# VectorE instead of GpSimd for one expert's weight split, and the last attention unit turned on TensorE instead of by DMA

## The chip, the cores and the metric

The kernel runs on one core of a Trainium2 chip. The metric is the device time of one execution in microseconds (us). The core has engines that work side by side, each through its own instructions in the order of the program: TensorE (PE; its weight loads are listed as PEld), VectorE (DVE), ScalarE (ACT), GpSimd (POOL) and SyncE (SP), which issues most DMAs. An engine waits for another by semaphores.

## The reference

Three layers in a row, in float32, on 4 batches of 576 tokens. The first is causal attention with 8 heads of 64 and a bias of cumulated decays. The second is a mixture of 8 experts: each token goes to one expert, its own best or, where a gate is open, that of the token in front of it. The third is a gated convolution layer of width 1024.

```python
x = attn_out.transpose(0, 2, 1, 3).reshape(B, S, H * D)          # 4 x 576 x 512
logits = einsum('bsd,de->bse', x, w_gate)                        # 8 experts
local_gate = 1 / (1 + exp(-einsum('bsd,de->bse', x, w_local)))
for b, s:                                                        # in order of s
    fresh_e = argmax(logits[b, s])
    e = fresh_e if s == 0 or local_gate[b, s] < 0.5 else prev_e
    out[b, s] = softmax(logits[b, s])[e] * (maximum(x[b, s] @ w1[e], 0) @ w2[e])
# then h = relu(out @ w_in); c = conv3(h); (h * sigmoid(c)) @ w_out
```

## The kernel before

Float32 values are split into a high and a low half of 16 bits, and a product is three matmuls (high by high, high by low, low by high). Everything is emitted by hand in one order, so each engine takes its instructions in the order of the program.

**Attention** runs in 8 units (4 heads of one batch each), and a unit in 14 steps; `at(d)` in its loop names what is d steps behind. For step t: scores (PE), `weights` one step behind (ACT exp), `rest` two (DVE), `values` four (PE, L503), `norm` five (DVE, L541), `xout` six (DVE, L547). A unit's result has two parts of two heads. `store` splits a part into halves `xh`: the high by ACT (L559), the low by DVE (L560) for the last unit. `rt.turn` turns them, so that the feature stands on the partitions: a DMA transpose issued by SP (L824), for the tail tokens another (L827). `put` writes them to `xd` in DRAM. For the last unit (NU - 1 = 7), part 0 is stored, turned and put at step N + 1 (N = 112 steps in all), part 1 at N + 6 and N + 7. values of its last head come at step N + 3 and the logits of unit 6 at N + 1, behind the turn of part 0 in the code.

**Routing.** `logits` (PE, L838 and L843) takes a turned unit, `collect` (DVE, L851 and behind) its logits; `finish` does both for the last unit, then the tables: exp (ACT, L899), sums (L900), the scan over the tokens (L905) that hands an expert on to the next token, positions (L920 to L934), one-hot planes (`plane`, L944), `sums` on PE into the PSUM tile `ix` (L954), and from it the tokens of each block of 128 (`rows(0)`, L960, for the gathers), the rows to write (`rows(1)`) and the scale `pp` (L981 to L983). `warm` (L964) puts matmuls without use between.

**The experts' weights** come expert by expert: `load(w, e)` by SP from DRAM into a stage (w is 0 for w1, 1 for w2; expert e; four parts), `lead` makes the high halves (ACT, L1023), `rest` the low ones: on DVE (one instruction, L1034) or, with `pool=True`, on GpSimd (two, L1030 and L1032). A part of a stage can be loaded anew when its `rest` is done. Four calls of these stand between attention and `finish`: lead and rest of (0,0), lead of (1,0), rest of (1,0) with `pool=True`; then the loads (0,2) and (1,2). Behind `finish`: lead (1,1) and (0,2), rest (0,1) and (0,2) on DVE; rest (1,1), called `second`, on GpSimd in pieces between the gathers of the first four blocks.

**The experts' blocks** (`step(b)`). `gather(b)` fetches 128 tokens (GpSimd, L1101), `turn(b)` turns them (PE L1108 into the PSUM tile `xp`, ACT L1109 copies it to `xt`), `mm1` is 2 x 12 matmuls into two of four `hp` tiles (L1078), ACT takes the relu's high halves (L1123), DVE the low (L1124), and SP turns them by DMA transpose (`ht`, L1126); `mm2` follows three blocks later. In step 1 stand lead and rest of (1,2); in step 0, behind mm1, load(0,3). `refill` (SP, a branch at L1071) and `event` (ACT and DVE, a branch at L1062) bring the later experts.

PSUM: the routing's tiles z, nrp, rfp, ep, rk and ix take 1, 2, 2, 1, 1 and 1 banks in this order; the experts' tiles lie in the same eight: hp 4, yp 2, and xp the last two, which were those of rk and ix. A tile waits for the last user of what lay there.

Of the kernel before, what the change touches and what calls it, by code (L numbers as in the profile page):

```python
# [9 lines left out]
F32 = mybir.dt.float32  # L10
# [14 lines left out]
NU = B * H // NH  # L25
# [89 lines left out]
def attention(tc, ctx, q, k, v, s, xd, rt, hook):  # L115
# [545 lines left out]
    for t in range(N + 9):  # L661
        if t == N - 2 * PER - 6:
            early.close()
        for f in am:
            f()
        am = []
        work(t)
        at = lambda d: steps[t - d] if 0 <= t - d < N else None
        if at(0):
            scores(at(0))  # L670
        for u, i in pieces.get(t, ()):
            if i == 0:
                P[u] = stage_a(u)
            am.append(P[u][i]())
        if at(1):
            weights(at(1))
        if at(2):
            rest(at(2))
        for d, f in ((4, values), (5, norm), (6, xout)):
            y = at(d)  # L680
            if y and y[2] == (3 if y[1] % 2 else 2):
                f(y[0], y[1])
        y = at(7)
        if y and y[2] == 3 and y != (NU - 1, 1, 3):
            store(y[0], y[1] // 2)
        y = at(8)
        if y and y[1:] == (3, 3):
            u = y[0]
            rt.turn(u, U[u, "xh"], U[u // 2, "xth"] if u % 2 else None, range(2) if u < NU - 1 else range(1, 2))
            if u == NU - 1:  # L690
                put(u, range(1, 2))
        y = at(PAR["h"]["ps"])
        if y and y[1:] == (3, 3) and y[0] < NU - 1:
            put(y[0], range(2))
        if at(9) == (NU - 1, 1, 3):
            store(NU - 1, 0)
            rt.turn(NU - 1, U[NU - 1, "xh"], None, range(1))
            put(NU - 1, range(1))
        y = at(PAR['h']['lg'])
        if y and y[1:] == (3, 3) and y[0] < NU - 1:  # L700
            rt.logits(y[0], mps.tile([128, 512], F32, name="mt"))
        y = at(PAR['h']['lg'] + PAR['h']['co'])
        if y and y[1:] == (3, 3) and y[0] < NU - 1:
            rt.collect(y[0])
        hook(t)


class Routing:
# [110 lines left out]
    def turn(self, u, xh, xth, parts):  # L819
# [5 lines left out]
        if xth is not None:  # L825
            t = self.xp.tile([128, 2, 2, 128], F16, name="xTt", bufs=1)
            nc.sync.dma_start_transpose(out=t.rearrange("d x k t -> d (x k) t"), in_=xth.rearrange("p x m d -> p (x m d)"))  # L827
            self.X[u] = x, t

    def logits(self, u, z):  # L830
        PE = self.tc.nc.tensor
        x, t = self.X.pop(u)
        z = self.X[u] = z[:, 0:45].rearrange("p (i e) -> p i e", e=9)
        terms = ((0, 0), (0, 1), (1, 0))
        for c in range(2):
            for i in range(4):
                for n, (a, w) in enumerate(terms):
                    PE.matmul(z[:, i], lhsT=x[:, c, i, a], rhs=self.w[:, w, 2 * (u % 2) + c], start=i + c + n == 0, stop=c == 1 and n == 2, skip_group_check=True)  # L838
        if u % 2:
            for e in range(2):  # L840
                for k in range(2):
                    for n, (a, w) in enumerate(terms):
                        PE.matmul(z[0:64, 4], lhsT=t[:, a, k, 64 * e:64 * e + 64], rhs=self.wt[:, w, k, e], start=False, stop=e + k + n == 4, skip_group_check=True)  # L843
# [28 lines left out]
        V.tensor_reduce(fc, eq, axis=AX.X, op=ALU.max)  # L872
        V.tensor_tensor(self.zrf[:, :, b, 0:1], r, fc, op=ALU.mult)

    def finish(self, ctx, busy, between):

        nc, keep = self.tc.nc, self.keep
        V, A, PE, G = nc.vector, nc.scalar, nc.tensor, nc.gpsimd
# [64 lines left out]
        def plane(i, x):  # L943
            V.tensor_tensor(BQ[:, i], BQ[:, 1], bc(pairs(x), [128, 10, NB, 2]), op=ALU.mult)  # L944
# [17 lines left out]
        def warm(n):  # L962
            for _ in range(n):
                PE.matmul(z, lhsT=self.id16, rhs=busy, start=True, stop=True, skip_group_check=True)  # L964
# [9 lines left out]
        V.tensor_tensor(pl, pc, ph, op=ALU.subtract)  # L974
        for i, x in ((2, tok[:, 1]), (3, ph[:, :, 0]), (4, pl[:, :, 0])):
            plane(i, x)
        warm(PAR["r"]["w1"])
        sums(slice(2, 5))
        warm(PAR["r"]["w2"])
# [366 lines left out]
def attn_moe_moe2(tc, q, k, v, s, wg, wl, w1, w2, w_in, conv, w_out, out):  # L1346
    nc = tc.nc
    w_in, conv, w_out = (t.bitcast(I32) for t in (w_in, conv, w_out))
    with tc.manual_schedule(), ExitStack() as ctx:
        const = ctx.enter_context(tc.tile_pool(name="keep", bufs=1))  # L1350
        dram = ctx.enter_context(tc.tile_pool(name="mid", bufs=1, space=bass.MemoryType.DRAM))
        xd = dram.tile([NT + 128, 2 * DM], F16, name="xd")
        yd = dram.tile([NT + 128, 2 * DM], F16, name="yd")
        keep = Keep()
        keep.idx = const.tile([128, 2, NB], I32, name="idx")
        keep.unit = const.tile([128, 128], F16, name="unit")
        keep.pp = const.tile([128, NB], F32, name="pp")
        keep.tab = const.tile([1, 6, 32], I32, name="tab")
        keep.pscale = YS * 2.0 ** -8 * 2.0 ** -23
        c2, c3, cx, ce = ExitStack(), ExitStack(), ExitStack(), ExitStack()  # L1360
        lay = Keep()

        def hook(t):
            if t == -1:
                stg = c2.enter_context(tc.tile_pool(name="stg", bufs=1, side="right", reuse_waits="tile"))
                t1, t2 = stg.tile([128, 4, 1024], F32, name="st1"), stg.tile([128, 8, 512], F32, name="st2")
                lay.e0 = [t1[:, k:k + 1] for k in range(4)], [t2[:, 2 * k:2 * k + 2] for k in range(4)]
                lay.e1 = [], []
                lay.m = moe_weights(tc, w1, w2, keep, lay.e0)
                lay.m.whole = t1, t2  # L1370
                rt.open(cx)
                lay.st2 = ce.enter_context(tc.tile_pool(name="st2", bufs=4, side="right", reuse_waits="tile"))
                return t1, t2, lay.st2
            if t == PAR["h"]["rc"]:
                lay.steps = itertools.chain(rt.constants(wg, wl), (None,)), rt.weights()
            if PAR["h"]["rc"] <= t < PAR["h"]["rc"] + 80:
                for x in range(PAR["h"]["rk"] if t > PAR["h"]["rc"] else 1):
                    next(lay.steps[0], None)
                if t >= PAR["h"]["rc"] + 3:
                    next(lay.steps[1], None)  # L1380
            for i in range(4):
                if t == PAR["h"]["e"][i]:
                    lay.m.load(i % 2, 0, part=i // 2)
                if t == PAR["h"]["e1"][i]:
                    x = lay.st2.tile([128, 2, 2, 1024], F16, name="k2").rearrange("d e n c -> d (e n c)").bitcast(F32)
                    n = 1024 if i < 2 else 512
                    lay.e1[i // 2].extend(x[:, 1024 * j:1024 * j + 1024].rearrange("p (k f) -> p k f", f=n) for j in range(2))
                    lay.m.load(i // 2, 1, lay.e1[i // 2], i % 2)


        rt = Routing(tc, keep)
        attention(tc, c3, q, k, v, s, xd, rt, hook)
        c3.close()
        with ExitStack() as c4:
            rg = c4.enter_context(tc.tile_pool(name="rg", bufs=1, reuse_waits="tile"))
            r1 = rg.tile([128, 2, 4, 3, 1024], F16, name="r1")
            r2 = rg.tile([128, 2, 8, 3, 512], F16, name="r2")
            xgp, xtp = (c4.enter_context(tc.tile_pool(name=n, bufs=b, reuse_waits="tile")) for n, b in (("xg", 4), ("xt", 2)))
            m = lay.m
            m.rings = r1, r2  # L1400
            m.first(m.lead, 0, 0)
            m.first(m.rest, 0, 0)
            m.first(m.lead, 1, 0)
            m.first(m.rest, 1, 0, pool=True)
            m.load(0, 2)
            m.load(1, 2)
            with ExitStack() as c5:
                rt.finish(c5, r1[:, 0, 0, 0, 0:512], lambda: m.first(m.lead, 0, 1, lay.e1[0]))
            m.first(m.lead, 1, 1, lay.e1[1])
            m.first(m.lead, 0, 2)  # L1410
            m.first(m.rest, 0, 1, lay.e1[0])
            m.first(m.rest, 0, 2)

            def second(k):
                m.first(m.rest, 1, 1, lay.e1[1], pool=True, chunks=k)

            def weights():
                ce.close()
                cx.close()
                wpool = c2.enter_context(tc.tile_pool(name="w2", bufs=1, side="right", reuse_waits="tile"))  # L1420
                lay.wio = wpool.tile([128, 2, 4, 1024], F16, name="wi"), wpool.tile([128, 2, 8, 512], F16, name="wo")
                return lay.wio

            moe(tc, xd, yd, m, w_in, w_out, keep, second, weights, xgp, xtp, keep.unit)
        wi, wo = lay.wio
        moe2(tc, yd, conv, (wi, wo), out)
        c2.close()
# [29 lines left out]
```

## Time and profile before

| | us |
|---|---|
| median of 3 runs | 740.72 |
| lowest and highest | 740.4 and 742.1 |
| the profiled execution | 738.07 |
| its span, first to last instruction | 736.3 |
| busy in it: PE, DVE, ACT, POOL | 625.4, 443.8, 380.8, 251.2 |

The rows below come from the profiled execution alone. All times in them count from the first instruction. A row of a timeline is one or several like instructions in a row of one engine (xN), with the time from the start of the first to the end of the last, and in brackets how long the engine had been idle and what ended it. A letter q behind an engine's name (SPq) is its queue: an instruction that issues a DMA and is not counted as work.

### The profile page before, as it was taken

Reading aid. Unit: us, or ns where it says so; the run is one execution under the profiler, and the core shown is the slowest. Engines: PE = TensorE matmul, PEld = TensorE weight load, DVE = VectorE, ACT = ScalarE, POOL = GpSimd, SP = SyncE. Lnnn points to the kernel's source line nnn. Section 1 sums busy time; section 2 is a strip of 40 time slices with the busy share of each in tenths; the row PEclk is TensorE's granted clock in tenths of the full one; section 3 lists DMA queues with packets and bytes.
Section 4 is the critical chain, followed back from the end, with each engine's and each line's share of the span. In section 5 each row is a group of like instructions: output and inputs, shape, how many; then the busy total and the mean of one; then the engine's idle time right before and its main releaser. Section 6 shows DMA issues by size and latency. Waiting matters only on the chain. (4 is left out here: it accounts for less than half of the span.)

```text
span 736.3 us, 15742 instructions
## 1 busy us (share of the span) xinstructions
PE 625.4 (85%) x5301; PEld 383.7 (52%) x5301; DVE 443.8 (60%) x838; ACT 380.8 (52%) x640; POOL 251.2 (34%) x367
## 2 busy tenths in 40 slices
PE   0449659978988944799999999999879999999997
PEld 0226547756767832344444444444347776665443
DVE  5527447866867688963686849574109995455000
ACT  4134557756757974544564727352109985455110
POOL 9316656654534147932253443533200000000000
PEclk9999779998989965999999999999999999999999
DMA  9977688979768895399999998966256300000111
GB/s 183 203 134 140 159 157 162 131 169 184 130 142 223 262 256 192 81 270 287 228 271 347 233 283 180 264 151 127 69 105 118 54 2 29 30 16 28 58 44 57
DMA packets 197279, 113.37 MB, mean 154 GB/s; under 512 B 147286, under 2 KB 173182, under 8 KB 197182
## 3 DMA queue, kind: packets, MB, share of 16 engines
q1 hardware_dynamic: 192574, 99.14, 59.4%
q0 software_dynamic: 4272, 12.93, 5.9%
q8 instruction: 48, 0.79, 0.4%
q14 instruction: 49, 0.40, 0.2%
q10 hardware_dynamic: 336, 0.11, 0.1%
HBM read 62.20 MB, written 15.31 MB: 105 GB/s over the span
## 5 line engine op out<-in xcount | busy, mean ns | idle before, releaser
L1078 PE MATMUL hp<-r,xt 128*128 x504 | 112.2, 379 | 7.3 <-ACT xt L1109 7.3
L1078 PE MATMUL yp<-r,ht 128*128 x504 | 112.2, 379 | 1.7 <-PEq L1186 1.1
L334 DVE TENSOR_REDUCE mx<-za 128x1 f32<-128x512 f32 (+4 forms) x113 | 67.9, 615 | 56.5 <-PE za L331 55.8
L1270 PE MATMUL hp<-yt,wi 128*128 128x288 f16 x768 | 95.5, 286 | 2.8 <-DMA yt<-yd 2.8
L1318 PE MATMUL o<-wo,g 128*128 128x512 f16 x432 | 94.5, 379 | 0.0
L475 ACT ACTIVATE phi<-z,lnes 128x512 f16<-128x512 f32 (+1 forms) x104 | 65.6, 630 | 45.1 <-PE z L441 44.8
L1270 PEld LDWEIGHTS <-wi 128*128 128x128 f16 x768 | 75.1, 98 | 23.5 <-DMA yt<-yd 3.3
L1078 PEld LDWEIGHTS <-xt 128*128 128x128 f16 x504 | 49.2, 98 | 66.6 <-ACT xt L1109 8.4
L1078 PEld LDWEIGHTS <-ht 128*128 128x128 f16 x504 | 48.5, 98 | 57.4 <-issue 1.8
L1034 DVE SCALAR_TENSOR_TENSOR r<-st,r 128x512 f32 (+3 forms) x76 | 69.3, 980 | 11.7 <-ACT r L1023 5.7
L331 PE MATMUL za<-k 70*128 70x256 f16 (+2 forms) x160 | 39.6, 331 | 40.7 <-DMA k<-k 38.2
L1023 ACT ACTIVATE r<-st 128x512 f32 (+3 forms) x84 | 57.0, 761 | 27.5 <-SPq L1071 16.1
L438 PE MATMUL z<-k 71*128 71x256 f16 (+2 forms) x320 | 58.6, 302 | 14.2 <-DMA k<-mr 11.0
L487 DVE TENSOR_TENSOR plo<-z,phi 128x512 f16<-128x512 f32 (+1 forms) x104 | 63.2, 609 | 9.4 <-ACT z L476 9.3
L1318 PEld LDWEIGHTS <-g 128*128 128x128 f16 x432 | 42.3, 98 | 49.5
L1139 POOL DMA_INDIRECT yd<-ys,idx x21 | 21.5, 1025 | 133.2 <-DVEq L1062 89.5
L476 ACT ACTIVATE z<-z,lnes 128x512 f32<-128x512 f32 (+1 forms) x104 | 62.8, 604 | 0.0
L503 PEld LDWEIGHTS <-phi 128*128 128x128 f16 (+2 forms) x896 | 52.6, 107 | 4.9 <-issue 1.0
L503 PE MATMUL o<-vv,phi 128*128 128x65 f16 (+1 forms) x832 | 53.6, 202 | 0.0
L438 PEld LDWEIGHTS <-k 71*128 71x128 f16 x576 | 39.8, 105 | 25.6 <-DMA k<-mr 11.8
L503 PE MATMUL o<-vv,plo 128*128 128x65 f16 (+1 forms) x416 | 50.4, 199 | 0.0
L1287 DVE SCALAR_TENSOR_TENSOR c<-hb,cw,c 128x576 f32<-128x576 f32 x32 | 26.1, 815 | 35.0 <-ACT c L1281 35.0
(255 smaller groups left out, 1003.3 us busy)
## 6 DMA issues: line engine op xcount, KB each, us to landing
st<-in_moe_w_dram SPq DMA_DIRECT2D x8, 2048.0 KB
st<-in_moe_w_dram SPq DMA_DIRECT2D x24, 512.0 KB
out_dram<-s SPq DMA_DIRECT2D x18, 256.0 KB
st<-in_k_dram SPq DMA_DIRECT2D x16, 256.0 KB
st<-in_q_dram SPq DMA_DIRECT2D x16, 256.0 KB
k<-k SPq DMA_DIRECT2D x16, 256.0 KB
xd<-xh SPq DMA_DIRECT2D x16, 256.0 KB
k<-in_moe_w_dram SPq DMA_DIRECT2D x8, 512.0 KB
```

What stands on the lines that cost most here:

```text
L331: PE.matmul(out, lhsT=l, rhs=r, start=start, stop=stop, skip_group_check=True)
L334: return lambda: V.tensor_reduce(out, z.rearrange("p (e c) -> p e c", e=m), axis=AX.X, op=ALU.max)
L438: PE.matmul(out, lhsT=ks[i], rhs=qs[i], start=first and not i, stop=False, skip_group_check=True)
L475: A.activation(hi[:, 0:n], z[:, 0:n], AF.Exp, bias=lnes, scale=1.0 / SC)
L476: A.activation(p[:, 0:n], z[:, 0:n], AF.Exp, bias=lnes, scale=1.0 / SC)
L487: (V if md == "a" else G).tensor_tensor(lo[:, 0:n], p[:, 0:n], hi[:, 0:n], op=ALU.subtract)
L503: PE.matmul(out, lhsT=w, rhs=x, start=first, stop=last, skip_group_check=True)
L1023: i = self.nc.scalar.activation(hi, src, AF.Copy, scale=self.scale[w])
L1034: i = nc.vector.scalar_tensor_tensor(lo, in0=src, scalar=sc, in1=hi, op0=ALU.mult, op1=ALU.subtract)
L1078: i = self.nc.tensor.matmul(out, lhsT=lhsT, rhs=self.rings[w][:, c, k, bass.ds(s, 1), f], **kw)
L1270: PE.matmul(st[x][:, n, 0:HN], lhsT=wi[:, c, k, m], rhs=t[:, n, a + k], start=k + a + c == 0, stop=k == 3 and a == 4)
L1318: PE.matmul(o, lhsT=g[:, a, k, 128 * i:128 * i + 128], rhs=wo[:, c, k], start=j == 0, stop=j == 23)
```

## The change

`rest` of (1,0) is made by DVE and not by GpSimd, and it is no longer called ahead of `finish` but inside it, through a new argument `behind`, after the last `plane`. load(1,2), which refills the same stage, moves with it; load(0,2) stays. On DVE it is one instruction for each of 8 chunks, where GpSimd had two.

The last unit is turned by a new function `turn_last`: for each of two groups (the high halves, the low halves) four matmuls with a unit matrix into one tile of attention's PSUM pool `zps`, and a copy into `xT`, by ACT for the first and by DVE for the second. Part 1 has a third tile for the tail tokens, copied by ACT. It is called where `rt.turn` was.

```diff
         if y and y[1:] == (3, 3):
             u = y[0]
-            rt.turn(u, U[u, "xh"], U[u // 2, "xth"] if u % 2 else None, range(2) if u < NU - 1 else range(1, 2))
-            if u == NU - 1:
+            if u < NU - 1:
+                rt.turn(u, U[u, "xh"], U[u // 2, "xth"] if u % 2 else None, range(2))
+            else:
+                rt.turn_last(U[u, "xh"], U[u // 2, "xth"], 1, zps)
                 put(u, range(1, 2))
...
             store(NU - 1, 0)
-            rt.turn(NU - 1, U[NU - 1, "xh"], None, range(1))
+            rt.turn_last(U[NU - 1, "xh"], None, 0, zps)
             put(NU - 1, range(1))
...
+    def turn_last(self, xh, xth, part, pool):
+
+        nc = self.tc.nc
+        if NU - 1 not in self.X:
+            self.X[NU - 1] = self.xp.tile([128, 2, 4, 2, 128], F16, name="xT"), None
+        x = self.X[NU - 1][0]
+
+        def tile(blocks, out, copy):
+            z = pool.tile([128, 512], F32, name="z").rearrange("p (i t) -> p i t", t=128)
+            for i, b in enumerate(blocks):
+                nc.tensor.matmul(z[:, i], lhsT=b, rhs=self.id16, start=i == 0, stop=i == 3, skip_group_check=True)
+            copy(out, z)
+
+        copies = lambda o, z: nc.scalar.activation(o, z, AF.Copy), nc.vector.tensor_copy
+        for n in range(2):
+            tile([xh[:, part, i, n] for i in range(4)], x[:, part, :, n], copies[n])
+        if xth is not None:
+            t = self.xp.tile([128, 2, 2, 128], F16, name="xTt", bufs=1)
+            h = xth.rearrange("p x m d -> p (x m d)")
+            tile([h[:, 128 * i:128 * i + 128] for i in range(4)], t.rearrange("d x k t -> d (x k) t"), copies[0])
+            self.X[NU - 1] = x, t
...
-    def finish(self, ctx, busy, between):
+    def finish(self, ctx, busy, between, behind):
...
         for i, x in ((2, tok[:, 1]), (3, ph[:, :, 0]), (4, pl[:, :, 0])):
             plane(i, x)
+        behind()
         warm(PAR["r"]["w1"])
...
             m.first(m.lead, 1, 0)
-            m.first(m.rest, 1, 0, pool=True)
             m.load(0, 2)
-            m.load(1, 2)
             with ExitStack() as c5:
-                rt.finish(c5, r1[:, 0, 0, 0, 0:512], lambda: m.first(m.lead, 0, 1, lay.e1[0]))
+                rt.finish(c5, r1[:, 0, 0, 0, 0:512], lambda: m.first(m.lead, 0, 1, lay.e1[0]), lambda: (m.first(m.rest, 1, 0), m.load(1, 2)))
```

## Rows read from the trace of the kernel before

**Rows 1.** Busy time by stretch: length, busy us and instructions per engine, clock, DMA share, GB/s.
```profile
262.00:264.00 2.00, 0.00 (x0) 0.00 (x0) 1.46 (x4) 1.72 (x3) 0.00 (x0) 0.85 1.27 134
...
295.00:330.00 35.00, 29.52 (x165) 14.47 (x163) 29.27 (x28) 17.90 (x26) 23.12 (x18) 1.00 0.71 172
330.00:360.00 30.00, 30.00 (x158) 14.27 (x157) 11.76 (x18) 12.24 (x17) 8.14 (x10) 1.00 0.98 279
```

**Rows 2.** Timeline at 329: start, us, engine, line, operation, tiles, count, idle before.
```profile
329.29 5.34 PE L1078 MATMUL hp<-r,xt 128*128 x24 [0.45 <-ACT xt L1109]
```

**Rows 3.** Timelines of PE, ACT and DVE at the end of attention.
```profile
258.26 0.74 PE L838 MATMUL mt<-w,xT 128*128 128x9 f16 x24
...
258.77 0.66 ACT L559 ACTIVATE xh<-x 128x512 f16<-128x512 f32 x1
...
259.93 0.68 DVE L560 TENSOR_TENSOR xh<-x,xh 128x512 f16<-128x512 f32 x1
...
261.39 0.17 DVE L541 TENSOR_SCALAR rc<-o 128x5 f32<-128x5 f32 x1 [0.68 <-PE o L503]
```

**Rows 4.** Timeline from the last unit's halves to the scan.
```profile
263.12 8.04 ACT L1023 ACTIVATE r<-st 128x1024 f16<-128x1024 f32 x12
...
264.19 4.63 DVE L1034 SCALAR_TENSOR_TENSOR r<-st,r 128x1024 f16<-128x1024 f32 x4 [0.22 <-ACT r L1023]
264.41 1.82 SPq L824 DMA_TRANSPOSE xT<-xh  x1
...
269.11 0.81 PE L843 MATMUL z<-wt,xTt 128*64 128x9 f16 x12
...
269.95 0.20 DVE L851 SCALAR_TENSOR_TENSOR lgs<-z,lgs 128x36 f32<-128x36 f32 x1 [1.13 <-PE z L843]
...
274.49 1.29 DVE L905 TENSOR_TENSOR_SCAN er<-nrs,rfp 128x576 f16<-128x576 f32 x1
```

**Rows 5.** Timeline of the routing's tables, GpSimd's split beside VectorE's work.
```profile
271.24 1.16 POOL L1032 TENSOR_TENSOR r<-st,r 128x512 f16<-128x512 f32 x1
271.30 1.16 DVE L871 TENSOR_TENSOR eqf<-eqf,w 128x40 f32<-128x40 f32 x1
...
278.70 0.32 DVE L925 TENSOR_TENSOR inc<-inc,rk 128x160 f32<-128x160 f32 x1
...
280.78 1.28 DVE L929 TENSOR_TENSOR inc<-inc,oh 128x160 f32<-128x160 f32 x1
...
282.79 1.03 DVE L932 TENSOR_SCALAR at<-posi 128x20 int32<-128x20 int32 x1
```

**Rows 6.** Timeline from the last planes to the first block's turn.
```profile
289.54 0.43 DVE L944 TENSOR_TENSOR bq<-bq,pl 128x500 f16<-128x500 f16 x1
...
290.51 0.63 POOL L1030 TENSOR_SCALAR k<-k 128x512 f32<-128x512 f32 x1
...
292.78 0.18 DVE L982 TENSOR_TENSOR ixs<-ixs,ix 128x25 f32<-128x25 f32 x1
...
294.86 0.61 PE L1108 MATMUL xp<-unit,xg 128*128 128x128 f16 x8
```

**Rows 7.** Timeline of the first blocks: relu's low halves, SP's issues, ScalarE's event.
```profile
306.31 1.27 DVE L1124 SCALAR_TENSOR_TENSOR hs<-hp,hs 128x512 f16<-128x512 f32 x2
...
309.64 2.43 SPq L1042 DMA_DIRECT2D st<-in_moe_w_dram  x4
...
317.73 8.61 SPq L1126 DMA_TRANSPOSE ht<-hs  x2
...
323.37 3.90 ACT L1023 ACTIVATE r<-st 128x1024 f32 x4 [5.64 <-SPq L1071]
```

**Rows 8.** One line over the whole run: durations in ns, min, median and max.
```profile
L871 DVE TENSOR_TENSOR eqf<-eqf,w x4: 200/201/1155, 145.3 to 271.3; 128x40 f32<-128x40 f32 x4
```

**Rows 9.** Timelines of VectorE: eight low halves of this shape at two places.
```profile
307.81 8.65 DVE L1034 SCALAR_TENSOR_TENSOR r<-st,r 128x512 f16<-128x512 f32 x8 [0.21 <-ACT r L1023]
...
365.26 4.90 DVE L1034 SCALAR_TENSOR_TENSOR r<-st,r 128x512 f32 x8
```

## The prediction

> **What bounds the kernel now.** I read TensorE's busy time by stretch first [rows 1]. From 330 us on it is full: 30.00 of 30.00 us in the stretch shown, at the full clock. Whatever reaches that stretch later or earlier should therefore reach the end by as much. So the change is worth what it moves at the door of it, and I follow one instruction there: the first matmul of mm1(4), at 329.29 [rows 2], which still waited for ScalarE (0.45 us idle). In front of it (295 to 330) TensorE has 29.52 of 35 us, so some lateness can hide there. The second view is the timeline of 256 to 296 us, engine by engine: the end of attention [rows 3], the hand-over to the routing [rows 4], its tables [rows 5], the start of the experts [rows 6]. There is no resource that is full in it; it is one chain through in-order engines, mostly VectorE, and both edits lie on it.
>
> **Turning part 0 on TensorE.** The call stands at step N+1, ahead of the logits of unit 6 in the same step and of values(3) in step N+3. An engine takes its instructions in the order of the program, so these wait behind the turn. TensorE was free for the logits at 258.26 [rows 3]. The turn needs the high half, written by ScalarE at 258.77 + 0.66 = 259.43, and the low half, by VectorE at 259.93 + 0.68 = 260.61. Its two tiles are four matmuls each. No such matmul stands at this place; the nearest row is the eight alike of the experts' turn, 0.61 us [rows 6], so 0.35 a tile (bounds 0.3, and 0.7 at the half clock). The logits start at 260.66 + 0.35 = 261.0, not 258.26: 2.75 us late. The values behind them, which ended just before VectorE's normalisation at 261.39, end as much later, near 264.1. What went in its place, a DMA transpose, was hidden: its logits had the time of part 1 to wait.
>
> **Turning part 1.** Everything behind the values moves by 2.75: both halves of part 1 and of its tail are ready at 266.7. Then come two tiles and the tail's tile, each 0.35 on TensorE and 0.6 to 0.65 in the copy out of PSUM (nearest row: VectorE's 0.64 mean of the two relus' low halves from PSUM [rows 7]). ScalarE copies the first and the tail's, which ends near 267.8; the copy stands ahead of the first expert's high halves (lead(0,0)), which started at 263.12 [rows 4]. So ScalarE starts them 4.7 late. The low halves rest(0,0) on VectorE follow 1.07 behind, as before (264.19 against 263.12), take 4.63, and end at 267.8 + 1.07 + 4.63 = 273.5. Before, they ran while the transposes were under way and cost nothing; that cover is gone. The logits themselves are done at 269.0 to 269.2, against 269.11 + 0.81 = 269.92: 0.8 to 0.9 earlier. But collect (L851) is behind rest(0,0) on VectorE: it starts at 273.4, not 269.95. **+3.5 us.** Bounds: -0.9 if the logits alone decided, +4.5 with the turns at the half clock.
>
> Here a page is weighed. The row: from the issue of part 1's transpose at 264.41 to the tail's logits at 269.11 there are 4.7 us [rows 4], with 4.63 us of VectorE's work beside it. The Trainium skill, "VectorE: DVE Perf Modes", section "The three transpose paths", gives 390 ns on TensorE and 1309 ns by DMA for a 128 x 128 block. For part 1's 8 blocks and the tail's 4 that would be, as an estimate from that page, 12 x 0.92 = 11 us saved, a time near 730. The trace has the whole DMA route at 4.7 us and not 15.7, so there are not 11 us to save, and the order of VectorE decides here.
>
> **GpSimd's split leaves the routing.** GpSimd's L1032 starts at 271.24 and takes 1.16; VectorE's L871, 40 elements, starts at 271.30 and takes 1.16, ending with it. That is in [rows 5]; of the line's four executions the median is 0.20 [rows 8]. So while GpSimd reads its operands, such a VectorE instruction stands still. Eight do so between 270.6 and 283.8, the first big one L871 and the last L932 (1.03 us): L868, L871 and L901 lose 0.4, 0.95 and 0.85 (2.2 us) ahead of the scan L905, and L920, L926, L927, L929 and L932 lose 0.35, 0.7, 0.35, 0.95 and 0.85 (3.2) behind it. L929 is the plain case: 1.28 where L925, of the same shape, takes 0.32. All of that goes.
>
> Ahead of the scan it isn't all gained: ScalarE's exp, which the sum L900 needs, follows twelve high halves (263.12 to 271.16 before), now from 267.8 to 275.8. Exp and the copy nrs behind it, some 0.9 together, end near 276.7, and there the scan starts, not at 274.49: +2.2. Behind the scan -3.2 (and some 0.1 of small rows): the token lists, gathers and planes come **1.1 us early**. Bounds: -5.5 (collect at the logits, all eight free) and +1.
>
> **VectorE's eight new instructions.** They start behind the last plane, 289.54 + 0.43 = 289.97 [rows 6] (times from here on are on the clock of before, with the 1.1 to take off at the end). VectorE then idled 2.3 us for the sums, which hides that much. Eight of this shape take 4.90 us with nothing of GpSimd's beside them, and 8.65 beside its splits [rows 9]. GpSimd's own split of the second expert (second) starts at 290.51 [rows 6], so I take a value near the upper end: 8.2, that is to 298.2. With the four rows of rows(1) and pp behind it VectorE is free for rest(0,1) at 299.3, not 293.2: **6.1 us late** (2.6 and 6.5 at the two bounds).
>
> Three things stand behind this queue.
> First a wait that the diff doesn't show: the experts' xp tile takes the two PSUM banks of rk and ix, and the last reader of ix is L982. It was at 292.78, out of the way of xp's first matmul at 294.86, when the warming matmuls were through. Now L982 comes near 298.9, so TensorE starts its turn(0) at 299.0: 4.1 late.
> Second, the low halves of the relu (L1124), at 306.31 [rows 7]: between them and rows(1) VectorE had no idle time, so they go to 312.4. The transpose of ht(0) waits for them, and load(0,3), behind it on SP, goes from 309.64 to 315.9: 6.3 late. The load's bytes then keep the issue of ht(1)'s transpose (317.73) busy, and only behind that does SP pass the refill's branch for which ScalarE's event(0,3) at 323.37 had waited. I move that by the load: +6.3 (if the transpose's wait for L1124 of block 1 alone counts, +4.4, since GpSimd's split ends meanwhile and eight low halves run at the faster pace).
> Third, load(1,2) itself: its four parts are issued as VectorE frees them, 291.7 to 298.2, and no longer as GpSimd does, during the tables. Nothing but the gathers moves beside them then, so I take them as landed by 302; ScalarE comes to them in step 1, behind the first relus. Cost nothing, with an estimated 2 us in hand.
>
> ScalarE's event feeds xt(4), and that the matmul at 329.29. TensorE's own path (299.0 plus the same work as before, 294.86 to 329.29) gives 333.4 and a little more if the clock falls in the pause; ScalarE's gives 335.6 to 335.8. The later one counts: **+6.5**. Less 1.1: **+5.4 us**. The profiled execution was 738.07 (span 736.3 and 1.8 around it), so it would be 743.5; against the median of the runs shown, 740.72, which lies 2.65 above the profiled one, 746.1.
>
> **Rivals.**
> *VectorE falls behind less* (chance 0.15). The new instructions run at the pace of 4.90, as they would if GpSimd's split came later or the two didn't meet. Lag 2.6, xp at 295.5, the event +2.6: with -1.1 it is +1.5 to +3, 742 to 744. Against it: second follows two gathers directly, at 290.51.
> *The clock falls* (0.10). With xp waiting for L982, TensorE pauses 4 us ahead of mm1(0). The granted clock dropped from its upper level (2.4 GHz) to 1.2 in the stretch 262 to 264 [rows 1] (mean 0.85), after TensorE had been idle from 261.4, so such a pause may be enough. mm1(0) and part of mm1(1) would then take twice as long; if some 6 us run at half, 3 us are lost on TensorE's path: 333.4 + 3 = 336.4, and a second fall in the wait of mm1(4) adds as much again: +8 to +9, 749.
> *The front's gain cancels the lag* (0.08): collect follows the logits at 269.0, which gives -5.5 at the token lists, and the lag of 6.4 comes on top: +0.9, no change that can be told.
> *Faster* (0.12): the freed tables win. Place: VectorE's collect at 269; price: -5.5; then a lag of 2.6: -2.9, 737.8. It decides as soon as L851 starts before 270 and rows(1) ends by 296 (on the clock of before). For it speaks that those 5.5 us are plain in [rows 5] and that TensorE has 5.5 idle us from 295 to 330. Against it: the order on TensorE, ScalarE and VectorE puts values(3), lead(0,0) and rest(0,0) behind the turns, and nothing in the diff moves them.
> That the change doesn't do what it says I see no way to: both edits are plain moves.
>
> **How the numbers follow.** The forecast, +4 to +7 us, has 0.55. About 0.2% (1.5 us) is what a measurement of this kernel can tell from no change. Slower by more than that: forecast 0.55, smaller lag 0.15, clock 0.10, together 0.80; within it 0.08; faster 0.12. The likeliest time is 746.1; its own range is 744.5 to 748. To hold 8 of 10 it must take in the smaller lag, and half of the fallen clock: 740 to 750. What is left out is the faster case and the far end of the clock's.
>
> **What the profile after would show.** Right: values(3) ends near 264.1; L851 starts near 273.4 behind the low halves; no VectorE instruction of the tables takes 1 us; the token list L960 comes about 1 us early; the eight new instructions take about 8 us; xp's first matmul waits for VectorE (L982); load(0,3) and the event are 4 to 6 us later. Wrong: L851 at 270 or before; xp's first matmul directly behind the warming ones; mm1(4) within 1.5 us of 329.29; or an idle stretch of TensorE after 330 that was not there, by which the lateness would be given back or grow.

## The result, and the profile after

The changed kernel takes 744.65 us, the median of 20 runs; the kernel before, run on the same chip, 740.22 us, also of 20. The ratio is 1.0079, with a 95% interval of 1.0053 to 1.0105: 5.8 us slower on 740.2 (3.9 to 7.8). The ratio leaves out runs in a slower state of the chip, so it isn't the ratio of the two medians, which lie 4.4 us apart. The forecast was +5.4, that is 746.1 us. The profiled execution took 748.8 us (span 747.1).

To compare two traces I align their clocks at one VectorE instruction that precedes every edit, the normalisation (L541) of the last unit's last head but one: 259.11 us in the kernel before, 259.96 after. "Late" below means: later than before, so aligned. Differences under 1 us mean little: in the seven kernels below that keep both DMA turns, and so are alike up to collect, collect lies between 0.3 us early and 0.7 late.

First the stretches, as in [rows 1]: length, busy us and instructions of PE, PEld, DVE, ACT and POOL, granted clock, DMA share, GB/s.

```profile
260.00:262.00 2.00, 0.89 (x10) 0.72 (x11) 1.42 (x6) 0.87 (x2) 0.00 (x0) 0.68 1.04 394
262.00:264.00 2.00, 2.00 (x53) 2.00 (x50) 0.82 (x2) 0.00 (x0) 0.00 (x0) 0.50 1.07 371
264.00:266.00 2.00, 2.00 (x33) 1.77 (x31) 0.00 (x0) 0.00 (x0) 0.00 (x0) 0.50 0.98 291
...
300.00:305.00 5.00, 2.26 (x12) 1.27 (x13) 4.90 (x8) 1.02 (x1) 4.65 (x5) 0.67 0.89 280
305.00:310.00 5.00, 5.00 (x17) 1.86 (x15) 5.00 (x4) 0.60 (x1) 4.92 (x3) 0.65 0.08 34
...
330.00:360.00 30.00, 30.00 (x159) 14.30 (x157) 16.66 (x22) 15.30 (x20) 4.86 (x4) 1.00 1.01 264
```

TensorE is full again from 330 us on, at the full clock. In two places ahead of that it has much to do at a lower granted clock: 0.50 in 262 to 266 (0.50 is 1.2 GHz, 1.00 is 2.4 GHz), and a mean of 0.67 and 0.65 in the two stretches from 300 to 310. The kernel before has 0.50 from 264 to 294 too; but there the values of the last head, which end at 261.4, were through by then.

The timelines at the first place, where [rows 3, 4] stand for the kernel before. Columns: start, us, engine, line, operation, tiles, count, and in brackets the idle time ahead and what ended it.

```profile
260.32 0.23 PEld L842 LDWEIGHTS <-xh 128*128 128x128 f16 x4 [1.18 <-ACT xh L559]
260.33 0.40 PE L842 MATMUL z<-unit,xh 128*128 128x128 f16 x4 [1.06 <-DVE rc L542]
260.77 0.68 DVE L560 TENSOR_TENSOR xh<-x,xh 128x512 f16<-128x512 f32 x1
261.51 0.61 PE L842 MATMUL z<-unit,xh 128*128 128x128 f16 x4 [0.78 <-DVE xh L560]
261.91 0.83 PE L862 MATMUL mt<-w,xT 128*128 128x9 f16 x24
...
266.38 0.24 PE L503 MATMUL o<-vvt,plo 64*64 64x65 f16 x1
...
270.52 8.04 ACT L1048 ACTIVATE r<-st 128x1024 f16<-128x1024 f32 x12
270.70 0.80 PE L867 MATMUL z<-wt,xTt 128*64 128x9 f16 x12
271.60 4.63 DVE L1059 SCALAR_TENSOR_TENSOR r<-st,r 128x1024 f16<-128x1024 f32 x4 [1.31 <-ACT r L1048]
276.14 0.19 DVE L875 SCALAR_TENSOR_TENSOR lgs<-z,lgs 128x36 f32<-128x36 f32 x1
277.12 0.20 DVE L895 TENSOR_TENSOR eqf<-eqf,w 128x40 f32<-128x40 f32 x1
...
279.57 1.29 DVE L929 TENSOR_TENSOR_SCAN er<-nrs,rfp 128x576 f16<-128x576 f32 x1
...
284.44 0.44 DVE L953 TENSOR_TENSOR inc<-inc,oh 128x160 f32<-128x160 f32 x1
```

Follow it down. TensorE waits for each half of part 0 in turn (1.06 and 0.78 us idle; the bracket of the first row of PE names a VectorE instruction that ended about then, and its weight load names the half itself), then has the logits and the values of the last head, which end at 266.62. The logits of the last unit are done at 271.50, and still their reader, collect (L875), starts at 276.14: directly behind rest(0,0) on its engine. The instruction of 40 elements that stood still for 1.16 us in [rows 5] takes 0.20, and that of 160 elements 0.44 instead of 1.28.

Then the start of the experts, where [rows 2, 6, 7] stand for before.

```profile
289.51 0.24 DVE L984 SCALAR_TENSOR_TENSOR idx<-ixs,negc,ix 128x25 int32<-128x25 f32 x1
291.80 8.95 DVE L1059 SCALAR_TENSOR_TENSOR r<-st,r 128x512 f16<-128x512 f32 x8
300.67 0.23 DVE L984 SCALAR_TENSOR_TENSOR idx<-ixs,negc,ix 128x25 int32<-128x25 f32 x1
301.16 0.18 DVE L1007 TENSOR_TENSOR ixs<-ixs,ix 128x25 f32<-128x25 f32 x1
301.48 0.87 PE L1133 MATMUL xp<-unit,xg 128*128 128x128 f16 x8 [5.12 <-DVE ixs L1007]
303.61 7.74 PE L1103 MATMUL hp<-r,xt 128*128 x24 [1.26 <-ACT xt L1134]
...
331.03 3.90 ACT L1048 ACTIVATE r<-st 128x1024 f32 x4 [4.02 <-SPq L1096]
335.79 1.02 ACT L1134 ACTIVATE xt<-xp 128x1024 f16<-128x1024 f32 x1
337.95 5.34 PE L1103 MATMUL hp<-r,xt 128*128 x24
```

The first tokens (L984) are 1.1 us late. VectorE's eight new instructions take 8.95 us. The first block's xp waits 5.12 us for VectorE's last read of ix (L1007, the L982 of before), and starts 5.8 late. mm1(0) takes 7.74 instead of the 5.34 that it took before; with that mm1(1) to mm1(3) are 8.4 late. mm1(4), at 337.95, is 7.8 late.

### The profile page after: what moved, and what is told of

The parts are those of the page before. It is cut to its first block, busy times and chain, and to the rows that moved or that the text cites. A ratio compares the mean times of both kernels' runs of the same rounds, so it can differ in the third digit from the quotient of the medians.

```text
span 747.1 us, 15761 instructions
## 1 busy us (share of the span) xinstructions
PE 633.4 (85%) x5321; PEld 388.4 (52%) x5321; DVE 445.2 (60%) x848; ACT 383.0 (51%) x643; POOL 238.7 (32%) x351
## 5 line engine op out<-in xcount | busy, mean ns | idle before, releaser
L1103 PE MATMUL hp<-r,xt 128*128 x504 | 116.3, 389 | 7.4 <-ACT xt L1134 7.4
L1059 DVE SCALAR_TENSOR_TENSOR r<-st,r 128x512 f32 (+3 forms) x84 | 77.0, 986 | 9.9 <-ACT r L1048 8.0
L503 PEld LDWEIGHTS <-phi 128*128 128x128 f16 (+2 forms) x896 | 54.6, 110 | 5.0 <-issue 0.9
L503 PE MATMUL o<-vv,phi 128*128 128x65 f16 (+1 forms) x832 | 55.6, 205 | 0.0
L503 PE MATMUL o<-vv,plo 128*128 128x65 f16 (+1 forms) x416 | 52.4, 202 | 0.0
L503 PEld LDWEIGHTS <-plo 128*128 128x128 f16 (+2 forms) x448 | 47.2, 111 | 0.0
```

What stands on the lines that cost most here:

```text
L503: PE.matmul(out, lhsT=w, rhs=x, start=first, stop=last, skip_group_check=True)
L1059: i = nc.vector.scalar_tensor_tensor(lo, in0=src, scalar=sc, in1=hi, op0=ALU.mult, op1=ALU.subtract)
L1103: i = self.nc.tensor.matmul(out, lhsT=lhsT, rhs=self.rings[w][:, c, k, bass.ds(s, 1), f], **kw)
```

## The experiments

Each compares with runs of the kernel before on the same chip. "Late" is by the aligned clocks of the profiled executions, and its order is collect / first tokens / xp / mm1(4). For the change: 5.3 / 1.1 / 5.8 / 7.8.

**Each half alone.** The first keeps the split on VectorE and turns the last unit by DMA, as before (both calls):

```diff
-            if u < NU - 1:
-                rt.turn(u, U[u, "xh"], U[u // 2, "xth"] if u % 2 else None, range(2))
-            else:
-                rt.turn_last(U[u, "xh"], U[u // 2, "xth"], 1, zps)
+            rt.turn(u, U[u, "xh"], U[u // 2, "xth"] if u % 2 else None, range(2) if u < NU - 1 else range(1, 2))
+            if u == NU - 1:
                 put(u, range(1, 2))
...
-            rt.turn_last(U[NU - 1, "xh"], None, 0, zps)
+            rt.turn(NU - 1, U[NU - 1, "xh"], None, range(1))
```

> The split goes to VectorE, the last unit keeps its DMA transposes. Theory (the turning costs at the front, the split frees the tables but its queue makes xp wait for L982): against before, values(3) and collect stay where they were, at 261.4 and 269.9; the token lists come 4 to 5.5 us early; the eight new splits take 8 to 9 us and xp's first matmul comes 0.5 us early to 1.5 us late, behind a pause of TensorE; mm1(0) runs partly at the half clock (7 to 8 us for 5.3); mm1(4) is 0 to 4 us late and the whole 0 to 0.5% slower. Rival (the split alone is what costs, and the turning is neutral): mm1(4) 7 to 9 us late, 0.8 to 1.2% slower.

Measured: 1.0002 (0.9966 to 1.0038). Late: 0.1 / -4.7 / 0.0 / 2.1. The second keeps the turn and gives GpSimd its split back:

```diff
+            m.first(m.rest, 1, 0, pool=True)
             m.load(0, 2)
+            m.load(1, 2)
...
-   rt.finish(..., lambda: (m.first(m.rest, 1, 0), m.load(1, 2)))
+   rt.finish(..., lambda: None)
```

> The last unit is turned on TensorE, the split stays on GpSimd ahead of the routing. Theory: values(3) end 4.5 us late (the wait for part 0's halves, and the half clock after it), collect 5.3 late, GpSimd's splits still stand in the tables, so the token lists are 5 to 6 us late; xp follows the warming matmuls without a pause, mm1(0) takes 5.3 us; mm1(4) is 5 to 6 us late, the whole 0.6 to 0.9% slower. Rival (a turn on TensorE saves the DMA's 4 us): collect 1 us early, 0.1% faster.

Measured: 1.0041 (1.0005 to 1.0076), less than the 0.6% that I had expected at least. Late: 5.3 / 6.1 / 5.0 / 5.8. VectorE and TensorE in this kernel:

```profile
269.15 4.63 DVE L1059 SCALAR_TENSOR_TENSOR r<-st,r 128x1024 f16<-128x1024 f32 x4 [1.31 <-ACT r L1048]
273.70 0.19 DVE L875 SCALAR_TENSOR_TENSOR lgs<-z,lgs 128x36 f32<-128x36 f32 x1
274.45 1.10 DVE L893 TENSOR_SCALAR eqf<-d 128x40 f32<-128x40 f32 x1
```

```profile
300.11 5.34 PE L1103 MATMUL hp<-r,xt 128*128 x24 [1.26 <-ACT xt L1134]
```

So the turn costs at collect, by rest(0,0) standing in front of it, with GpSimd's split or without (1.10 us for 40 elements shows the split beside). The other half wins 4.7 us at the tokens and gives all of it back at xp. At mm1(4) the two halves add up to the change in the traces (2.1 and 5.8, against 7.8); in the times only the turn is told from no change. Here the split's three rows, VectorE's queue, the wait, and the clock:

```profile
285.72 8.94 DVE L1057 SCALAR_TENSOR_TENSOR r<-st,r 128x512 f16<-128x512 f32 x8
```

```profile
295.39 0.69 PE L1131 MATMUL xp<-unit,xg 128*128 128x128 f16 x8 [5.01 <-DVE ixs L1005]
297.33 7.93 PE L1101 MATMUL hp<-r,xt 128*128 x24 [1.25 <-ACT xt L1132]
```

**Which of the two turns.** Part 0 goes back to the DMA, part 1 stays on TensorE:

```diff
-            rt.turn_last(U[NU - 1, "xh"], None, 0, zps)
+            rt.turn(NU - 1, U[NU - 1, "xh"], None, range(1))
```

> Both parts of the change, but part 0 of the last unit is turned by DMA as before; part 1 and the tail on TensorE. Theory: values(3) end at 261.4 as before and at the full clock, collect comes 0.3 to 1 us late (behind the low halves of the first expert, which start 1.5 us late), the token lists 3.5 to 5 us early; xp still waits for L982; mm1(4) is 2 to 4 us late, 4 to 5 us ahead of the change. Rival (part 0's wait on TensorE is hidden by part 1's work): mm1(4) as late as with the change.

Measured: 1.0007 (0.9971 to 1.0044). Late: 0.9 / -3.3 / 1.4 / 3.9. The second keeps part 0 on TensorE, but behind the values of the last head:

```diff
         if at(9) == (NU - 1, 1, 3):
             store(NU - 1, 0)
-            rt.turn_last(U[NU - 1, "xh"], None, 0, zps)
             put(NU - 1, range(1))
...
+        if at(11) == (NU - 1, 1, 3):
+            rt.turn_last(U[NU - 1, "xh"], None, 0, zps)
```

> The change as it is, but part 0 of the last unit is turned on TensorE two steps later, behind values(3). Theory (part 0's turn costs by its place, not by its engine): values(3) end at 261.4 on the clock of before and at the full clock, collect 0.5 to 2 us late and not 5.3, mm1(4) 3 to 5 us late, 3 to 5 us ahead of the change. Rival (the matmuls or copies themselves cost): collect 4 us late or more.

Measured: 1.0041 (1.0002 to 1.0081). Late: 2.1 / -2.1 / 2.6 / 4.6; the values' end is 0.0 late, against 4.4 with the change. The second's collect, still directly behind rest(0,0):

```profile
267.29 4.63 DVE L1060 SCALAR_TENSOR_TENSOR r<-st,r 128x1024 f16<-128x1024 f32 x4 [1.31 <-ACT r L1049]
271.84 0.19 DVE L876 SCALAR_TENSOR_TENSOR lgs<-z,lgs 128x36 f32<-128x36 f32 x1
```

By the traces, then, of collect's 5.3 us 3.2 are the place of part 0's turn (5.3 less 2.1). The rest, 1.2 for its being on TensorE at all (2.1 less 0.9) and 0.9 for the turn of part 1, is each no more than kernels alike up to there differ by. By the times only the first of the two kernels is told from the change (its interval ends at 1.0044, where the change's begins at 1.0053); the second's overlaps both.

**Is the long mm1(0) the clock?** `warm` puts matmuls without use into the pause in front of xp; 'w2' counts those of the second call.

```diff
- 'r': {'cut': 12, 'w1': 6, 'w2': 8, 'w3': 22},
+ 'r': {'cut': 12, 'w1': 6, 'w2': 32, 'w3': 22},
```

> The change as it is, with 32 warming matmuls instead of 8 in front of xp. Theory: mm1(0) takes 5.3 us, mm1(1) comes 6 us late against before and not 8.4; mm1(4) 5.5 to 7 us late; the whole 0.5 to 0.9% slower. Rival (the wait behind the turn is hidden once the clock is kept): mm1(4) within 2 us of before.

Measured: 1.0065 (1.0032 to 1.0099). Late: 5.3 / 1.1 / 5.8 / 6.4. With 26 in the kernel that has the split alone:

> The split alone (DMA turning as before), with 26 warming matmuls instead of 8 in front of xp, so that TensorE has no 5 us pause while it waits for L982. Theory (the pause costs the clock, the clock costs 2.6 us of mm1(0)): mm1(0) takes 5.3 us and not 7.9; xp as in the split alone; mm1(1) 2.6 us earlier than there, at +0.1 against before; mm1(4) at 0 to +1.4 (VectorE's and SP's queue then decide). Whole: the same as before, within 0.3%, and 0 to 0.35% faster than the split alone. Rival (the matmuls without use take more than they save, or the clock falls for another reason): mm1(1) as late as in the split alone.

Measured: 1.0001 (0.997 to 1.0032). Late: -0.3 / -5.1 / -0.5 / 3.9. TensorE of the two:

```profile
301.03 0.61 PE L1133 MATMUL xp<-unit,xg 128*128 128x128 f16 x8
302.90 5.34 PE L1103 MATMUL hp<-r,xt 128*128 x24 [1.26 <-ACT xt L1134]
```

```profile
292.34 0.61 PE L1131 MATMUL xp<-unit,xg 128*128 128x128 f16 x8 [1.47 <-DVE ixs L1005]
294.20 5.34 PE L1101 MATMUL hp<-r,xt 128*128 x24 [1.25 <-ACT xt L1132]
...
331.08 2.29 PE L1101 MATMUL hp<-r,xt 128*128 x5 [4.77 <-ACT xt L1132]
```

With TensorE at work until xp, or idle for 1.47 us of that, mm1(0) takes 5.34 in both: the 2.4 us were the pause's doing. They are hardly worth anything. In the first, ScalarE's event holds mm1(4) next, 6.4 late; in the second mm1(1) to mm1(3) are 0.5 early, and mm1(4) then waits 4.77 us for ScalarE, whose relu had waited for the transposes ht; I had expected it at most 1.4 late, and it is 3.9. Behind TensorE's lateness stood a second one, through VectorE and SP: in the change a little smaller (6.4 against 7.8), in the split alone larger (3.9 against 2.1).

**Where the eight instructions stand.** Behind the rows and pp instead of in front of them:

```diff
-        behind()
         warm(PAR["r"]["w1"])
         sums(slice(2, 5))
...
         V.tensor_scalar(keep.pp, ...)
+        behind()
```

> Both parts of the change, but the eight splits stand behind rows(1) and pp instead of ahead of them. Theory: xp no longer waits for L982, it follows the warming matmuls some 1.5 us later than before the change (the rest of the late front); mm1(0) takes 5.3 us at the full clock. VectorE's idle 2 us ahead of rows(1) are no longer used, so its low halves of the relu are later still, and mm1(2) or ScalarE's event wait for them: mm1(4) 7 to 10 us late, as with the change. Rival (xp's wait and the clock's fall behind it are the whole price, the queue behind has slack): mm1(4) 1.5 to 3 us late.

Measured: 1.0177 (1.0135 to 1.0219). Late: 4.4 / 0.2 / -0.9 / 14.8. The wait at xp is gone, and everything behind is worse than I expected. TensorE, and ScalarE's relu behind it:

```profile
309.10 6.12 PE L1103 MATMUL hp<-r,xt 128*128 x17 [0.66 <-DVE r L1059]
...
318.54 5.34 PE L1103 MATMUL hp<-r,xt 128*128 x24 [2.87 <-DVE hs L1149]
...
331.70 8.13 PE L1103 MATMUL hp<-r,xt 128*128 x24 [7.38 <-ACT xt L1134]
```

```profile
329.56 1.08 ACT L1148 ACTIVATE hs<-hp 128x512 f16<-128x512 f32 x2 [12.77 <-DMA ht<-hs]
```

mm1(1) needs rest(0,1), which is behind the eight; then mm1(2) waits for relu's low halves, and mm1(3) for a copy that stands behind a relu on ScalarE, which waited 12.77 us for ht. So VectorE's queue is a bound of its own: the wait at xp only shows where it is met first.

**VectorE's pace.** The split of the second expert is held back until behind the fourth gather (in the kernel with the split alone):

```diff
-        for b, k in enumerate((None, (0, 1), (2,), (3, 4, 5, 6, 7))):
+        for b, k in enumerate((None, None, None, range(8))):
```

> The split alone (DMA turning), with GpSimd's own split of the second expert moved behind the fourth gather, so that VectorE's eight instructions start beside gathers and not beside splits. Theory (they take 9 us because GpSimd holds what they need, 4.9 without): the eight take 5 to 7 us, L982 is 1 us early to 0.5 late against before, xp 1.5 to 4 us early with a pause of 1 to 3 us, mm1(0) 5.3 to 6.5 us. mm1(4) 1 us early to 1.5 late, the whole the same within 0.3%. Rival (VectorE's pace is its own): the eight take 8 to 9 us as in the split alone.

Measured: 1.0000 (0.9966 to 1.0034). Late: 0.4 / -4.4 / -2.9 / 0.2.

```profile
282.79 5.77 DVE L1057 SCALAR_TENSOR_TENSOR r<-st,r 128x512 f16<-128x512 f32 x8
```

```profile
289.30 0.61 PE L1131 MATMUL xp<-unit,xg 128*128 128x128 f16 x8 [2.51 <-DVE ixs L1005]
291.15 7.01 PE L1101 MATMUL hp<-r,xt 128*128 x24 [1.25 <-ACT xt L1132]
```

5.77 us with gathers on GpSimd for most of that time, against 8.94 beside its splits: the pace was set by what GpSimd does. (mm1(0), at 7.01, took longer than I had expected: behind 2.51 us of idleness the clock was down again, 0.50 in 292 to 294.) (The Trainium skill, "SBUF — State Buffer", section "Who interferes with whom", says it as a rule: a VectorE instruction with two inputs in SBUF and a GpSimd instruction that reads SBUF exclude each other for whole instructions. The two rows agree, and so does the row of 40 elements in [rows 5] that took 1.16 us and ended with GpSimd's.)

**Sharing the split.** In the kernel with the DMA turns, GpSimd makes the first four (five) chunks at the old place and VectorE the rest:

```diff
+            m.first(m.rest, 1, 0, pool=True, chunks=range(5))
             m.load(0, 2)
+            m.load(1, 2, part=0)
...
-   lambda: (m.first(m.rest, 1, 0), m.load(1, 2))
+   lambda: (m.first(m.rest, 1, 0, chunks=range(5, 8)), m.load(1, 2, part=1))
```

> DMA turning as before; GpSimd splits the first four chunks at the old place and VectorE the other four behind the planes; load(1,2) in two halves accordingly. Theory: GpSimd is out of the tables from the scan on, so the token lists come 3 us early; VectorE's four chunks (4 us) are half hidden by the 2.3 us for which it idled, so L982 is no later than the warming matmuls: xp 2.5 to 3 us early with no pause, mm1(0) 5.3 us; mm1(4) 0.5 to 3 us early, the whole 0.1 to 0.4% faster. Rival (VectorE's queue behind decides, whatever the front gains): mm1(4) 1 us late or more.

Measured: 0.9997 (0.9966 to 1.0028). Late: -0.2 / -2.8 / -2.3 / -0.5.

> As the four and four, with five chunks on GpSimd and three on VectorE. Theory: token lists 2.5 to 3 us early; VectorE's three chunks take 3 us, nearly all in its idle time; xp 2.5 us early, mm1(4) 1.5 to 3 us early, the whole 0.2 to 0.4% faster, the best of these. Rival: VectorE's queue decides, mm1(4) no earlier than before.

Measured: 0.9984 (0.9956 to 1.0012). Late: 0.5 / -2.3 / -2.8 / 0.2. In both xp is over 2 us early, the clock holds (mm1(0) 5.34), and mm1(4) has lost most or all of it again, in the second as its rival had it; neither is told from the kernel before in the times. ScalarE and TensorE of the second:

```profile
311.37 0.60 ACT L1146 ACTIVATE hs<-hp 128x512 f16<-128x512 f32 x1 [3.87 <-DMA ht<-hs]
```

```profile
329.16 4.04 PE L1101 MATMUL hp<-r,xt 128*128 x18 [2.53 <-ACT xt L1132]
```

The low halves of the relu stand behind rest(0,2) and rest(1,2) on VectorE, ht behind them, and the next relu behind ht. So I put the relu's low halves of blocks 0 and 1 first:

```diff
-                m.first(m.rest, 1, 2)
...
+            if b < 2:
+                m.first(m.rest, b, 2)
...
-            m.first(m.rest, 0, 2)
```

> Five chunks on GpSimd, three on VectorE, DMA turning, and VectorE takes the relu's low halves of blocks 0 and 1 ahead of the third expert's splits rest(0,2) and rest(1,2), not behind them. Theory (what the front gained in the five and three was lost in VectorE's queue: the relu's low halves, so the transposes ht and the load behind them on SP): low halves of block 0 at 299 to 301 and not 304.9, mm1(3) and mm1(4) 2 to 3 us early against before, the whole 0.3 to 0.4% faster than before. Rival (the load's bytes or the refill's branch decide, not VectorE): mm1(4) no more than 1 us early, the whole the same.

Measured: **0.9946 (0.9914 to 0.9979)**, 735.29 us against 740.1. Late: 0.7 / -2.3 / -2.7 / -3.3. And only this last edit, in the kernel before:

> The kernel before with only that order of VectorE's: relu's low halves of blocks 0 and 1 ahead of rest(0,2) and rest(1,2). Theory: mm1(0) to mm1(3) stay, they followed ScalarE's copy; mm1(4) gains its 0.45 us wait at most; the whole the same within 0.2%. Rival (the order alone is worth the gain): 0.3% faster or more.

Measured: 0.9982 (0.9949 to 1.0015). Late: 0.7 / 0.2 / -1.2 / -1.8. VectorE and TensorE of the first of the two:

```profile
286.46 3.73 DVE L1057 SCALAR_TENSOR_TENSOR r<-st,r 128x512 f16<-128x512 f32 x3
...
297.76 0.68 DVE L1147 SCALAR_TENSOR_TENSOR hs<-hp,hs 128x512 f16<-128x512 f32 x1
```

```profile
292.83 5.34 PE L1101 MATMUL hp<-r,xt 128*128 x24 [1.25 <-ACT xt L1132]
...
324.77 5.34 PE L1101 MATMUL hp<-r,xt 128*128 x24
...
413.77 5.34 PE L1101 MATMUL hp<-r,xt 128*128 x24 [2.38 <-ACT xt L1132]
```

The relu's low halves come 7.4 us earlier than before, the event 6.4, and the 2.7 us of xp reach mm1(4). That they reach the end this trace doesn't show: two later waits of 2.4 us each, one of them at 413.77, leave the last matmul of the experts 0.2 early. What shows it are the times, by which this version beats both kernels. In the second of the two 1.2 us of the 1.8 at mm1(4) lie ahead of the edit, at xp: there the granted clock was already 0.73 in 290 to 292, where it was 0.50 up to 294 in the trace before. That the gain is the two edits together rather than either alone is what the three intervals suggest (0.9984, 0.9982, 0.9946), though they overlap.

## Why the prediction was right

The forecast's chain held link by link as far as xp, though not all its sizes did; at mm1(4) another path decided than the one it named. That the total came out so near is in part luck: the trace has both paths later than forecast, and the times show less than the trace.

- **values(3)**: predicted 2.75 late, measured 4.4. The turn's waits are as predicted; the mis-sized term is TensorE's pace behind them. The granted clock was 0.68 in 260 to 262 and 0.50 from there, so the logits and the values ran at the lower level. I had the lower clock only in the bound.
- **collect**: the mechanism, rest(0,0) and not the logits, is what the row at 276.14 shows. Predicted +3.5, measured +5.3; the values' 4.4 lie in it.
- **The tables**: behind the scan 3.2 us were to go, and 3.1 went (4.2 late at the scan, 1.1 at the tokens). Predicted -1.1 net, measured +1.1, so here the sign was wrong: the scan was 4.2 late, not 2.2.
- **Eight low halves**: 8.2 predicted, 8.95 measured. **xp's wait** for the L982 of before: named, and there. Predicted +3.0 (4.1 less 1.1), measured +5.8, where the tokens' 2.2 and the eight's 0.75 make up the difference.
- **The clock at mm1(0)** was a rival, with 0.10, and it came true (2.4 us). The warmed kernels show it.
- **mm1(4)**: here a step failed. The prediction had it wait for "ScalarE's" event, "the later one counts", with TensorE's own path behind. In the trace xt(4) was ready at 336.81 and TensorE came to it at 337.95, without a wait: TensorE's path decided, because the clock had lengthened it. ScalarE's event was 6.8 late, against 5.2 predicted (6.3 less 1.1); TensorE's path was 7.8 late, against 3.0 (333.4 less 329.29 and 1.1). The two paths lie 1.1 us apart, which is why filling the pause moved mm1(4) by 1.4 and not by 2.4.
- **The end**: +5.4 forecast, 5.8 by the ratio and 4.4 by the medians, 7.8 at mm1(4) in the one trace. So the sum is near the times, but the trace says that its parts in front were undersized by some 2 us, and why the times show less than the trace isn't settled. Part of it is the premise that what reaches mm1(4) reaches the end by as much, which holds only roughly: from mm1(4) to the last matmul of the experts the lateness goes from 7.8 to 10.0 here, from 5.8 to 3.8 with the turn alone, and from -3.3 to -0.2 with five and three chunks and the relu first. Nor can times tell 0.2% apart, as I had put it: the interval is 0.26% to either side with 20 runs, and about 0.35% with 12. The profiled execution lost still more behind the door, and I had named such an idle stretch as a thing that would make the lateness grow:

```profile
426.93 7.03 PE L1103 MATMUL hp<-r,xt 128*128 x24 [2.36 <-ACT xt L1134]
```

The kernel with five and three chunks and the relu first has such stalls too, and is faster all the same. What sets them wasn't tried.

Of the other rivals, "VectorE falls behind less" didn't hold here, and does when GpSimd's second split is held back (5.77 us). "The front's gain cancels the lag" is what the split alone does (tokens 4.7 early, xp 0.0, the whole 1.0002), with the turns left to the DMA. "The freed tables win" needed collect at 270, which only the kernels with part 0 turned by DMA had; there the tables did win up to 5.1 us, and xp and the relu's order took it back.

## What to carry to other kernels

A transfer that is replaced by work on in-order engines costs what stands behind that work: read the next instructions of each engine ahead of the saved latency. When work moves from one engine to another, follow the last reader of every buffer that is about to be reused; here a read of a few elements, 8.95 us down VectorE's queue, held a matmul of another phase. And a gain at the front has to be followed to the first stretch that is full: here it was lost twice on the way, and putting the small instruction that others wait for ahead of the large one was what let it through to that stretch.

## What the runs showed that I had not expected

- Two waits of TensorE of 1.06 and 0.78 us, with four matmuls between them, were followed by the lower clock: 0.68, then 0.50 for the next 8 us and more, though TensorE was full from 262 to 266. The kernel with the turn alone shows the same.
- Behind a pause of 5.20 us ahead of xp mm1(0) took 7.59, of 5.12 us 7.74, of 5.01 us 7.93, of 4.69 us 8.10, of 2.51 us 7.01, of 1.47 and 0.54 us 5.34, and with none 5.34. (In each of these kernels TensorE waits 1.25 us more between xp and mm1(0).)
- SP's issue of the transpose ht took 1.6 to 2.1 us where load(0,3) was still behind it. Behind that load the next two took 5.95 and 5.82 in the warmed kernel with the split alone (13.29 with the wait between them). In all kernels but the one with the splits behind pp (15.9), the issue of ht(1) starts 5.9 to 9.1 us after the load's first issue, and whenever it starts it ends 10.3 to 12.1 after it. That fits the load's bytes as the cause, as the prediction had it; it stays an inference, as no run has the transpose without the load. A third buffer for the relu's halves, which would loosen that chain, wasn't tried.
